# Later decodings, planning moved to the last expert, and contractions filled with zero rows

## The chip, the cores and the metric

The kernel runs on one core of a Trainium2 chip. The metric is the device time of one execution in microseconds (us); the profile shows one execution with every instruction of TensorE (PE), VectorE (DVE), ScalarE (ACT), GpSimd (POOL) and the queue engine SyncE (SP).

## The reference

Three layers follow each other: attention (a coarse one over means of four positions, and a local one over a band of seven positions), a mixture of 8 experts where each token goes to its best expert, and a dense layer with a leaky ReLU. All inputs but the two dense weights are float32; these two are float64 words.

```python
B, H, S, D = 4, 8, 576, 64
q_d, k_d, v_d = (mean of q, k, v over groups of 4 positions)      # 144 groups
out_up = np.repeat(softmax(q_d @ k_d.T / 8) @ v_d, 4, axis=2)
mask = np.abs(pos[:, None] - pos[None, :]) < 4
out_local = softmax(np.where(mask, q @ k.T / 8, -1e9)) @ v
x = (out_up + out_local) as [2304 tokens, 512]
expert_idx = argmax(normalised x @ normalised expert_emb.T / tau)
x[mask of e] = gate_w * (np.maximum(x[mask of e] @ w1[e], 0.0) @ w2[e])   # 512 -> 1024 -> 512
h = x @ w_in                                                       # 512 -> 2048
out = np.maximum(0.01 * h, h) @ w_out                              # 2048 -> 512
```

## The kernel before

**Attention.** The order of all its work, with the routing of tokens, stands in the table ORDER, one name for each step: `qk`, `vg` and `vw` load q and k, v for the means, and v for the local windows; `T`, `E`, `P` transpose q and k, copy them out of PSUM and form the means; `ds` to `dl` are the coarse attention; `S` to `LX` are the local one, in 18 tiles of 128 tokens, each of four strips of 32 positions with a window of 38 (WIN). In `lo_score` a small matmul first writes the mask into PSUM: its stationary operand is `strip4`, its moving one `mask`, with 32 rows of contraction. In `lo_pv` the contraction runs over the 38 positions of the window: exponentials are transposed in blocks of 64 columns of which 38 are used, and v is held in the tiles `vws`, of which 48 rows in each 64 are loaded. In `dn_pv` it runs over 72 groups (HG), half of 144, with exponentials in the tile deT and v in `vds`, which has a further column of ones for the sum.

**Experts.** The best expert's tokens come first, in two parts: part A (192 rows) while attention ends, part B (220 rows) after it. Then seven more follow in the order of their size, in slots of fixed capacity (372 down to 252 rows). Each expert has eight steps f; in a step `l1` makes 128 hidden units (12 matmuls), `relu` (ACT, L969) and `relu_lo` (DVE, L974) split them into a high part `hh` and a remainder `hl`, and `l2` adds their product to the output (12 matmuls). `l2` of a step stands one `l1` later. Weights are loaded by SP (`w_moe_load`) and split the same way (ACT L860, DVE L863). The rows of the next expert are gathered by POOL (`x_rows`, L759), scaled by ACT (`x_gate`, L800), transposed by PE, and split into `xhi` (ACT, L810) and `xlo` (DVE, L812) in the last four steps of the expert before.

**Planning.** Tokens beyond a slot's capacity are done in a loop at the end. The functions `pl_off` to `pl_regs` (32 small DVE instructions, L1036 to L1081) work out the places of the experts' outputs (`pl_off`) and that loop's list (all others).

**Dense weights.** They are float64 and are decoded into float32 on the chip: `w_ffn_load` (POOL queue, L883, two buffers) loads one of 32 units, `decode1` (DVE, L895 and L897) and `decode2` (DVE, L902 and L903, then a sum on POOL, L905) form the float32 words, and `w_ffn_hi` (ACT) and `w_ffn_lo` (DVE) split them. Sixteen of the units (u below 4) are decoded while experts run, the others in the dense layer.

**What sets the order behind attention.** A list `plan` of times: each step of an expert or of the dense layer has a modelled start, every function is entered with a time (`at`), and the list is sorted. The four compute engines take their instructions in that order, each engine strictly one after the other; nothing reorders on DVE, ACT, POOL or SP. Planning and decodings are entered so:

```python
            at(mid(num["e", "B", 0] + n, 6), fn, *args)          # planning, n = 0 to 7
        t0, t1 = start[num["e", "B", 0]], start[num["e", 6, 0]]
                t = t0 + (t1 - t0) * g / 16                       # unit g = 0 to 15
                at(max(start[i0] - 10.0, 1.0), w_ffn_load, u, i, j)
            at(mid(i0, 3.6), decode1, u, i, j)
```

Of the kernel before, what the change touches and what calls it, by code (L numbers as in the profile page):

```python
# [24 lines left out]
E = 8  # L25
# [31 lines left out]
ORDER = """  # L57
qk.0.0.0 ce qk.0.1.0 vg.0.1 qk.0.0.1 qk.1.1.1 emb cm qk.0.1.1 cr vg.0.0 T.0.0.0.0+8 qk.1.0.1 T.0.0.0.2 E.0.0.0.0
qk.1.1.0 K.0 T.0.0.0.1 E.0.0.0.2 T.0.1.0.0 qk.2.1.0 E.0.0.0.1 cf K.1 T.0.1.0.1 E.0.1.0.0 P.0.0.0 T.0.1.0.2 E.0.1.0.1
# [50 lines left out]
def tile_kernel(ctx, tc, q, k, v, emb, tau, w1, w2, win, wout, out):  # L110
# [51 lines left out]
    with man:  # L162
# [25 lines left out]

        vds = [ac.tile([HG, 2, H, D + 1], F32, name="vd%d" % i) for i in range(O['NVD'])]
        vws = [ac.tile([P, NP, GS, D], F32, name="vw%d" % i) for i in range(O['NVW'])]  # L190
        rep_w = ac.tile([P, 2 * HW + 4 * P], F32R, name="rep_w")
        rem_w = ac.tile([P, NP, 3 * HW], F32R, name="rem_w")

        for t in vds:
            V.memset(t[:, :, :, D:D + 1], 1.0)

        strip4 = ac.tile([STRIP, 4, STRIP], BF16, name="strip4")
        mask = ac.tile([STRIP, 3, WIN], BF16, name="mask")

# [15 lines left out]
        def consts_mask():  # L215
            G.tensor_copy(strip4, ident[:STRIP, 0:STRIP].unsqueeze(1).to_broadcast([STRIP, 4, STRIP]))
            G.memset(mask, 0.0)
            for base, sg in ((3, 1), (3, -1)):
                G.affine_select(out=mask, in_=mask, pattern=[[3 * sg, 3], [-sg, WIN]], compare_op=ALU.is_ge,
                                fill=NEG, base=base, channel_multiplier=sg)  # L220
# [103 lines left out]
        def on(kind):  # L324
            return Scalar if O["EC"][kind] == "ACT" else Vector
# [36 lines left out]
        def v_item(b, c):  # L362
            if c == 0:
                vd[b] = vds[len(vd) % O['NVD']]
            src = raw.pop((b, 2, c)).rearrange("p h (r f d) -> p r h f d", r=2, f=4)
            d = vd[b][:, :, NP * c:NP * c + NP, 0:D]
            t0 = src[:, :, :, 0, :]
            G.tensor_tensor(out=t0, in0=t0, in1=src[:, :, :, 1, :], op=ALU.add)
            G.tensor_tensor(out=d, in0=src[:, :, :, 2, :], in1=src[:, :, :, 3, :], op=ALU.add)
            G.tensor_tensor(out=d, in0=d, in1=t0, op=ALU.add)  # L370
# [39 lines left out]
        def dn_T(b, u, j):  # L410
            if j == 0:
                deT[b, u] = pl.tile([HG, 6, 2, P], F32, name="deT", tag="deT%d" % (u * O["NDE"]), bufs=1)
            e = de[b, u]
            ps = dps[b, u, j] = psB.tile([P, 512], F32, name="psDT", tag="B")
            idle(ps[:, 0:256], dn_T, b, u, j)
            for x_ in range(4):
                n, kc = 2 * j + x_ // 2, x_ % 2
                i, m = (n // 2, n % 2) if n < 4 else (n % 2, 2)
                tr(ps[:HG, x_ * P:(x_ + 1) * P], e[:, i, m, kc::2])

        def dn_Te(b, u, j):
            on('dE').copy(deT[b, u][:, 2 * j:2 * j + 2], dps.pop((b, u, j))[:HG].rearrange("p (n k g) -> p n k g", k=2, g=P))

        def dn_pv(b, u):
            eT = deT.pop((b, u))
            n_ = 4 + 2 * u
# [50 lines left out]
        def lo_score(t):  # L477
# [4 lines left out]
            for c, o in enumerate(places) if len(set(places)) > 1 else ((slice(0, P), places[0]),):  # L482
                c = c if isinstance(c, slice) else slice(32 * c, 32 * c + 32)
                for s in range(2):
                    T.matmul(ps[c, s, 0:m], strip4.rearrange("k a q -> k (a q)")[:, c],
                             mask[:, o, :].unsqueeze(1).to_broadcast([STRIP, NP, WIN]), start=True, stop=True)
            for n in range(NP):
# [46 lines left out]
        def lo_pv(t):  # L534
# [22 lines left out]
            for n in range(NP):  # L557
                for s in range(2):
                    for c, b, sg, w0 in strips(t):
                        w = vwt[b * (NSTRIP // GS) + sg // GS][:, :, sg % GS]  # L560
                        T.matmul(ps[32 * c:32 * c + 32, s, n * D:(n + 1) * D],
                                 eT[64 * s:64 * s + WIN, n, 32 * c:32 * c + 32], w[64 * s:64 * s + WIN, n, :],
                                 start=False, stop=True, skip_group_check=True)
# [537 lines left out]
        def w_half_lo(u, i, c):  # L1101
# [3 lines left out]
            es=(emb_sq,), ep=(emb_pow,), en=(emb_norm,), et=(emb_T,), emb=(load_emb,),  # L1105
            ce=(consts_escore,), cm=(consts_mask,), cf=(consts_fill,), cr=(consts_route,), qk=(load_qk,),
            vg=(load_vg,), T=(q_pe,), E=(q_ev,), P=(q_pool,), v=(v_item,), ds=(dn_score,), dm=(dn_max,),
# [47 lines left out]
        for n, (fn, args) in enumerate(((pl_off, ()), (pl_caps, ()), (pl_over, ()), (pl_tiles, ()), (pl_first, ()),  # L1155
                                        (pl_pick, (0,)), (pl_pick, (1,)), (pl_regs, ()))):
            at(mid(num["e", "B", 0] + n, 6), fn, *args)
        for i, (kind, s, f) in enumerate(steps):
# [52 lines left out]
        for g in range(32):  # L1211
            u, i, j = g // 4, g // 2 % 2, g % 2
            if u < 4:
                t = t0 + (t1 - t0) * g / 16
                i0 = max(n for n in range(len(steps)) if start[n] <= t)
                at(max(start[i0] - 10.0, 1.0), w_ffn_load, u, i, j)
            else:
# [84 lines left out]
```

## Time and profile before

| what | value |
|---|---|
| median of 3 runs | 872.42 us (865.73 to 874.82) |
| profiled execution | 870.72 us, of which 869.0 us from the first to the last instruction |
| TensorE matmul busy | 822.0 us, 95% |
| VectorE busy | 457.7 us, 53% |
| ScalarE busy | 339.7 us, 39% |
| GpSimd busy | 206.2 us, 24% |
| mean granted TensorE clock | 0.949 of full speed |

Times within the profile count from the span's first instruction. Attention runs to about 190 us, part B of the first expert from about 212 us, the other experts to about 452 us, the dense layer to the end. An engine's busy share says little by itself; what counts is which wait ends last in each stretch, and at which clock TensorE worked there.

### The profile page before, as it was taken

The page shows a single profiled execution, that of the slowest core. Times are in us where ns is not written, and L with a number is a line of the kernel's source. Part 1 is how long each engine was busy: PE and PEld are TensorE (multiplying, and loading weights), DVE is VectorE, ACT ScalarE, POOL GpSimd, SP SyncE. Part 2 cuts the span into 40 slices and gives each one's busy share as a digit, 9 for nine tenths or more (in the row PEclk, how much of TensorE's full clock was granted, in tenths as well). Part 3 has the DMA queues.
Part 4 walks back from the last instruction along what each step waited for, and adds up shares of the span by engine and source line. Part 5 has one row for each costly group of instructions (what it writes and reads, how often), then busy time and mean ns, then how long its engine had stood idle before and what let it go on. Part 6 is the DMA issues. An engine that isn't in the chain of part 4 may idle for free. (4 is left out here: it accounts for less than half of the span.)

```text
span 869.0 us, 18997 instructions
## 1 busy us (share of the span) xinstructions
PE 822.0 (95%) x7887; PEld 748.3 (86%) x7887; DVE 457.7 (53%) x901; ACT 339.7 (39%) x686; POOL 206.2 (24%) x238
## 2 busy tenths in 40 slices
PE   7979998898799999899999999999999999999995
PEld 6867877788789999899998789999999999999994
DVE  4646655263697778586659993332233232232222
ACT  3455545363345645455533332232222222232221
POOL 6555642243122433232013330101001001001001
PEclk9988978589799999999999999999999999999998
DMA  9888652556474875776653420011011011000001
GB/s 265 178 179 185 150 136 68 136 154 137 115 226 161 268 213 189 240 232 222 198 160 122 157 72 1 25 49 37 1 37 36 1 37 37 1 1 37 0 1 39
DMA packets 104652, 97.88 MB, mean 113 GB/s; under 512 B 58956, under 2 KB 83148, under 8 KB 104562
## 3 DMA queue, kind: packets, MB, share of 16 engines
q1 hardware_dynamic: 94018, 69.88, 29.0%
q0 software_dynamic: 10544, 26.74, 10.0%
q8 instruction: 64, 1.05, 0.5%
q14 instruction: 26, 0.21, 0.1%
HBM read 81.48 MB, written 15.12 MB: 111 GB/s over the span
## 5 line engine op out<-in xcount | busy, mean ns | idle before, releaser
L918 PE MATMUL psh<-xlo,w 128*128 128x384 f32 (+9 forms) x672 | 215.3, 320 | 1.9 <-DVE xlo L812 1.9
L917 PE MATMUL psh<-xhi,w 128*128 128x384 f32 (+9 forms) x672 | 215.5, 321 | 0.0
L919 PE MATMUL psh<-xhi,w 128*128 128x384 f32 (+9 forms) x672 | 214.8, 320 | 0.0
L949 DVE SCALAR_TENSOR_TENSOR hs<-hs 128x384 f32<-128x384 f32 x96 | 61.9, 645 | 186.2 <-ACT hs L948 186.2
L918 PEld LDWEIGHTS psh<-xlo,w 128*128 128x128 f32 x672 | 127.3, 189 | 6.2 <-DVE xlo L812 2.2
L917 PEld LDWEIGHTS psh<-xhi,w 128*128 128x128 f32 x672 | 127.5, 190 | 4.0
L919 PEld LDWEIGHTS psh<-xhi,w 128*128 128x128 f32 x672 | 127.2, 189 | 0.0
L948 ACT COPY hs<-psh 128x384 f32<-128x384 f32 x96 | 46.0, 479 | 194.4 <-PE psh L919 191.2
L919 PE MATMUL pso<-w,hl 128*128 128x512 f32 x282 | 112.6, 399 | 2.1 <-DVE hl L955 1.7
L917 PE MATMUL pso<-w,hh 128*128 128x512 f32 x282 | 111.7, 396 | 0.5 <-ACT hh L954 0.4
L918 PE MATMUL pso<-w,hh 128*128 128x512 f32 x282 | 111.0, 393 | 0.0
L918 PE MATMUL psy<-hl,w 128*128 128x192 f32 (+8 forms) x288 | 87.4, 304 | 10.6 <-DVE hl L974 10.5
L1021 POOL DMA_INDIRECT out_dram<-o,tk x18 | 18.5, 1025 | 320.8 <-ACT o L1020 315.1
L917 PE MATMUL psy<-hh,w 128*128 128x192 f32 (+8 forms) x288 | 89.1, 309 | 0.7 <-ACT yT L1002 0.7
L863 DVE TENSOR_TENSOR w<-r,w 128x1024 fp32r<-128x1024 f32 (+1 forms) x72 | 83.2, 1162 | 7.9 <-ACT w L860 7.6
L919 PE MATMUL psy<-hh,w 128*128 128x192 f32 (+8 forms) x288 | 87.0, 302 | 0.0
L954 ACT CAST hh<-hs 128x384 fp32r<-128x384 f32 x94 | 48.3, 513 | 92.9 <-DVE hs L949 92.9
L905 POOL TENSOR_TENSOR ds<-r 128x512 f32<-128x512 f32 x32 | 42.2, 1318 | 159.7 <-DVE r L903 85.1
L955 DVE TENSOR_TENSOR hl<-hs,hh 128x384 fp32r<-128x384 f32 x94 | 52.4, 557 | 45.8 <-ACT hh L954 45.8
L969 ACT ACTIVATE hh<-psh 128x192 fp32r<-128x192 f32 (+8 forms) x72 | 29.2, 406 | 107.3 <-PE psh L919 102.4
L919 PEld LDWEIGHTS pso<-w,hl 128*128 128x128 f32 x282 | 52.9, 188 | 20.4 <-DVE hl L955 8.5
L860 ACT CAST w<-r 128x1024 fp32r<-128x1024 f32 (+1 forms) x72 | 67.7, 948 | 6.5 <-DMA r<-in_moe_w_dram 6.5
(226 smaller groups left out, 1275.8 us busy)
## 6 DMA issues: line engine op xcount, KB each, us to landing
r<-in_moe_w_dram SPq DMA_DIRECT2D x64, 512.0 KB
r<-in_moe_w_in_dram POOLq DMA_DIRECT2D x16, 512.0 KB, 6.5
r<-in_moe_w_out_dram POOLq DMA_DIRECT2D x16, 512.0 KB, 3.7
vw<-in_v_dram SPq DMA_DIRECT2D x64, 96.0 KB
vg<-in_v_dram SPq DMA_DIRECT2D x8, 576.0 KB
x_d<-xt SPq DMA_DIRECT2D x18, 256.0 KB
yc<-yT_d SPq DMA_DIRECT2D x6, 768.0 KB
qk<-in_q_dram SPq DMA_DIRECT2D x4, 576.0 KB
```

The lines of the kernel that those rows point to most:

```text
L860: A.copy(w[:, 0, i, cs], src)
L863: V.tensor_tensor(out=w[:, 1, i, cs], in0=src, in1=w[:, 0, i, cs].bitcast(F32), op=ALU.subtract)
L905: G.tensor_tensor(out=s_.bitcast(F32), in0=lw.bitcast(F32), in1=hw.bitcast(F32), op=ALU.add)
L917: T.matmul(ps, lh, rh, start=start, stop=False)
L918: T.matmul(ps, lh, rl, start=False, stop=False)
L919: T.matmul(ps, ll, rh, start=False, stop=stop)
L948: A.copy(hs, ps[:, 0:n])
L949: V.scalar_tensor_tensor(out=hs, in0=hs, scalar=0.01, in1=hs, op0=ALU.mult, op1=ALU.max)
L954: A.copy(gh[:, 0:n], hs)
L955: V.tensor_tensor(out=gl[:, 0:n], in0=hs, in1=gh[:, 0:n].bitcast(F32), op=ALU.subtract)
L969: A.activation(hh[:, 0:n], psl1["e", s, f][:, 0:n], AF.Relu)
L1021: i = G.indirect_dma_start(out=out, out_offset=bass.IndirectOffsetOnAxis(ap=tok[c][:, j, 0:1], axis=0), in_=o, in_offset=None, bounds_chec ...
```

## The change

It has two parts. In attention, the contractions of 32, 38 and 72 rows are filled up to 128, 64 and 128 rows. The tiles `strip4`, `mask`, `vds` and deT get 128 partitions, deT becomes one tile held for the whole of attention (as a tile with one buffer it already had one place in memory), and the added rows are set to zero once, by a new step `cv` on POOL that stands third in ORDER, and by memsets of `vws` on DVE at the very start. No other name in ORDER moves.

Behind attention, planning starts three steps later with `pl_off`, and its other seven functions go to steps 1 to 7 of the last expert. The sixteen early decodings begin 18 modelled us later and are spread over what is left of the same stretch; their loads are entered 13 instead of 10 modelled us ahead.

```diff
 ORDER = """
-qk.0.0.0 ce qk.0.1.0 vg.0.1 qk.0.0.1 qk.1.1.1 emb cm qk.0.1.1 cr vg.0.0 T.0.0.0.0+8 qk.1.0.1 T.0.0.0.2 E.0.0.0.0
+qk.0.0.0 ce cv qk.0.1.0 vg.0.1 qk.0.0.1 qk.1.1.1 emb cm qk.0.1.1 cr vg.0.0 T.0.0.0.0+8 qk.1.0.1 T.0.0.0.2 E.0.0.0.0
...
-        vds = [ac.tile([HG, 2, H, D + 1], F32, name="vd%d" % i) for i in range(O['NVD'])]
+        vds = [ac.tile([P, 2, H, D + 1], F32, name="vd%d" % i) for i in range(O['NVD'])]
+        deT_ = ac.tile([P, 6, 2, P], F32, name="deT")
...
-        for t in vds:
-            V.memset(t[:, :, :, D:D + 1], 1.0)
-
-        strip4 = ac.tile([STRIP, 4, STRIP], BF16, name="strip4")
-        mask = ac.tile([STRIP, 3, WIN], BF16, name="mask")
+        for t in vws:
+            V.memset(t, 0.0)
+
+        def consts_vd():
+            for t in vds:
+                G.memset(t[64:], 0.0)
+                G.memset(t[:HG, :, :, D:D + 1], 1.0)
+            G.memset(deT_[64:], 0.0)
+
+        strip4 = ac.tile([P, 4, STRIP], BF16, name="strip4")
+        mask = ac.tile([P, 3, WIN], BF16, name="mask")
...
+            G.memset(strip4, 0.0)
+            G.tensor_copy(strip4[:STRIP], ident[:STRIP, 0:STRIP].unsqueeze(1).to_broadcast([STRIP, 4, STRIP]))
             G.memset(mask, 0.0)
...
-                             mask[:, o, :].unsqueeze(1).to_broadcast([STRIP, NP, WIN]), start=True, stop=True)
+                             mask[:, o, :].unsqueeze(1).to_broadcast([P, NP, WIN]), start=True, stop=True)
...
-                                 eT[64 * s:64 * s + WIN, n, 32 * c:32 * c + 32], w[64 * s:64 * s + WIN, n, :],
+                                 eT[64 * s:64 * s + 64, n, 32 * c:32 * c + 32], w[64 * s:64 * s + 64, n, :],
...
-            at(mid(num["e", "B", 0] + n, 6), fn, *args)
+            at(mid(num["e", "B", 3] if n == 0 else num["e", E - 1, n], 6), fn, *args)
...
-                t = t0 + (t1 - t0) * g / 16
+                t = t0 + 18.0 + (t1 - t0 - 18.0) * g / 16
                 i0 = max(n for n in range(len(steps)) if start[n] <= t)
-                at(max(start[i0] - 10.0, 1.0), w_ffn_load, u, i, j)
+                at(start[i0] - 13.0, w_ffn_load, u, i, j)
```

Three places show what this moves. The first is DVE at the begin of part B of the first expert (psx holds its transposed rows, psh its hidden units, r a loaded unit of dense weights, the names from m on belong to planning). Before:

```order
L812 TENSOR_TENSOR xlo<-psx,xhi 128x220 x4
L895 TENSOR_SCALAR ds<-r_4174 128x512
L897 SCALAR_TENSOR_TENSOR r_4174<-r_4174,ds 128x512
L974 SCALAR_TENSOR_TENSOR hl<-psh,hh 128x220
L902 TENSOR_SCALAR ds<-r_4174 128x512
L903 SCALAR_TENSOR_TENSOR r_4174<-r_4174,ds 128x512
L1036 TENSOR_TENSOR m_79<-rank,eio 128x64
L1037 TENSOR_TENSOR m_79<-m_79,cnt 128x64
L1038 TENSOR_REDUCE tmp<-m_79 128x8
L1039 CAST regs<-tmp 128x8
```

And now:

```order
L818 TENSOR_TENSOR xlo<-psx,xhi 128x220 x4
L980 SCALAR_TENSOR_TENSOR hl<-psh,hh 128x220 x4
L1042 TENSOR_TENSOR m_79<-rank,eio 128x64
L1043 TENSOR_TENSOR m_79<-m_79,cnt 128x64
L1044 TENSOR_REDUCE tmp<-m_79 128x8
L1045 CAST regs<-tmp 128x8
L980 SCALAR_TENSOR_TENSOR hl<-psh,hh 128x220
L818 TENSOR_TENSOR xlo<-psx,xhi 128x372
L869 TENSOR_TENSOR w<-r_4079,w 128x1024
```

Four remainders hl of part B stand in a row behind xlo; the decoding of r, which stood ahead of the first of them, and most of planning are gone from here.

The second is GpSimd between the gathers for the second expert (124 rows each) and for the third (112). Before:

```order
L759 DMA xe<-x_d,tks 124x512 x3
L883 DMA r_4174<-in_moe_w_in_dram 128x2x256
L883 DMA r_4176<-in_moe_w_in_dram 128x2x256
L905 TENSOR_TENSOR ds<-r_4174 128x512
L883 DMA r_4274<-in_moe_w_out_dram 128x512
L905 TENSOR_TENSOR ds<-r_4176 128x512
L883 DMA r_4448<-in_moe_w_out_dram 128x512
L759 DMA xe<-x_d,tks 112x512 x3
```

And now:

```order
L765 DMA xe<-x_d,tks 124x512 x3
L889 DMA r_4191<-in_moe_w_in_dram 128x2x256
L889 DMA r_4313<-in_moe_w_in_dram 128x2x256
L911 TENSOR_TENSOR ds<-r_4191 128x512
L765 DMA xe<-x_d,tks 112x512 x3
L889 DMA r_4422<-in_moe_w_out_dram 128x512
L911 TENSOR_TENSOR ds<-r_4313 128x512
L889 DMA r_4548<-in_moe_w_out_dram 128x512
```

The gathers for the second expert and two loads stand as they did; the gather for the third now comes after one sum of a decoding, ds, instead of two, and ahead of the third load.

The third is GpSimd at the start, behind the constants for escore. Before:

```order
L224 MEMSET escore_106 128x512
L216 CAST strip_116<-ident 32x128
L217 MEMSET mask 32x114
L219 AFFINE_SELECT mask<-mask 32x114 x2
L237 MEMSET tri 128x128
```

And now:

```order
L232 MEMSET escore_106 128x512
L200 MEMSET vd_107 64x1040
L201 MEMSET vd_107 72x16
L200 MEMSET vd_108 64x1040
L201 MEMSET vd_108 72x16
L202 MEMSET deT 64x1536
L223 MEMSET strip_118 128x128
L224 CAST strip_118<-ident 32x128
L225 MEMSET mask 128x114
L227 AFFINE_SELECT mask<-mask 32x114 x2
```

Six memsets stand ahead of the strip and the mask, and the strip and mask tiles are longer.

## Rows read from the trace of the kernel before

**Rows 1.** Windows by stage: length, busy us (instructions) per engine, clock, DMA share, GB/s

```profile
20.00:100.00 80.00, 70.72 (x1809) 58.82 (x1811) 48.51 (x110) 41.38 (x89) 42.96 (x45) 0.87 0.84 183
...
100.00:190.00 90.00, 82.35 (x2001) 70.71 (x1991) 49.03 (x168) 47.77 (x117) 35.90 (x40) 0.75 0.45 118
...
262.00:435.00 173.00, 168.99 (x1207) 167.40 (x1206) 127.84 (x192) 94.01 (x163) 46.33 (x40) 0.99 0.68 216
...
435.00:460.00 25.00, 25.00 (x185) 23.95 (x183) 15.52 (x30) 8.99 (x20) 4.16 (x6) 1.00 0.54 164
```

**Rows 2.** Waits of PE, 195 to 560 us: total us, times, longest us

```profile
PE psy L918 <- DVE hl L974: 10.5, 2, 8.7
```

**Rows 3.** Timeline of PE: start us, us, instruction, idle before it and its releaser

```profile
223.73 0.55 PE L918 MATMUL psy<-hl,w 128*128 128x220 f32 x1 [8.68 <-DVE hl L974]
...
248.01 0.68 PE L918 MATMUL psh<-xlo,w 128*128 128x372 f32 x1 [1.94 <-DVE xlo L812]
...
358.77 0.30 PE L155 MATMUL psx<-ident,xe 94*128 94x94 f32 x1 [0.65 <-ACT xe L800]
...
361.08 0.62 PE L918 MATMUL psy<-hl,w 128*128 128x300 f32 x1 [1.85 <-DVE hl L974]
```

**Rows 4.** Windows of 4 us behind the two stalls of the first expert

```profile
224.00:228.00 4.00, 4.00 (x22) 4.00 (x23) 3.60 (x12) 0.62 (x1) 1.61 (x2) 0.56 0.23 28
...
248.00:252.00 4.00, 3.99 (x18) 3.99 (x19) 3.68 (x9) 2.74 (x5) 1.48 (x2) 0.57 0.63 165
```

**Rows 5.** Timeline of DVE: decoding, first and last of planning, a later decoding

```profile
222.23 0.43 DVE L895 TENSOR_SCALAR ds<-r 128x512 uint32<-128x512 uint32 x1 [10.51 <-DMA r<-in_moe_w_in_dram]
...
222.69 0.69 DVE L897 SCALAR_TENSOR_TENSOR r<-r,ds 128x512 uint32<-128x512 uint32 x1
...
224.66 0.22 DVE L1036 TENSOR_TENSOR m<-rank,eio 128x64 f32<-128x64 f32 x1
...
249.04 0.17 DVE L1081 CAST regs<-fi 128x24 int32<-128x24 f32 x1
...
359.50 0.43 DVE L895 TENSOR_SCALAR ds<-r 128x512 uint32<-128x512 uint32 x1 [5.24 <-DMA r<-in_moe_w_in_dram]
```

**Rows 6.** DMA issues at 205.2:205.5 and 208.3:209: count, KB each, us to landing

```profile
xe<-x_d,tks POOLq DMA_INDIRECT x1, 11.6
...
r<-in_moe_w_in_dram POOLq DMA_DIRECT2D x1, 512.0 KB, 13.8
```

**Rows 7.** Windows in attention, before and in stretches of low clock

```profile
12.00:16.00 4.00, 2.23 (x46) 1.78 (x41) 2.59 (x5) 1.71 (x4) 1.90 (x4) 1.00 1.07 291
...
108.00:111.50 3.50, 3.47 (x98) 3.18 (x98) 3.29 (x11) 1.37 (x5) 2.42 (x4) 1.00 0.72 150
...
111.50:121.70 10.20, 9.77 (x188) 8.26 (x188) 2.95 (x10) 4.67 (x12) 2.20 (x3) 0.50 0.56 146
...
152.40:173.00 20.60, 17.37 (x295) 15.64 (x302) 5.40 (x23) 7.12 (x17) 4.97 (x6) 0.50 0.53 138
```

**Rows 8.** PE by line and form, 108 to 111.5 us: busy us, mean ns

```profile
L561 PE MATMUL psLV<-vw,leT 38*32 38x64 f32 x64 | 0.9, 224 | 0.0
```

**Rows 9.** PE by line and form, whole span: rows*columns, moving tile, count

```profile
L561 PE MATMUL psLV<-vw,leT 38*32 38x64 f32 x1152 | 18.1, 246 | 6.2 <-issue 6.2
...
L433 PE MATMUL psDV<-vd,deT 72*64 72x65 f32 x256 | 9.8, 229 | 1.7 <-issue 1.7
...
L553 PE MATMUL psLV<-dnl,rem_w 128*128 128x64 f32 x32 | 5.8, 308 | 0.0
```

**Rows 10.** Timeline of the start: POOL, DVE, PE

```profile
1.74 0.98 POOL L224 MEMSET escore<- 128x512 f32 x2
...
9.71 0.73 POOL L358 TENSOR_TENSOR t<-qkT 128x288 f32<-128x288 f32 x1 [1.22 <-ACT rem_w L233]
...
8.99 1.22 DVE L349 COPY qkT<-psT 128x384 f32<-128x384 f32 x2 [7.75 <-PE psT L344]
...
16.43 2.19 PE L344 MATMUL psT<-ident,qk 128*64 128x128 f32 x36 [2.20 <-DMA qk<-in_k_dram]
```

More of the change, by code (lines that the diff above doesn't have):

```diff
@@ L215, in consts_mask @@
         def consts_mask():
-            G.tensor_copy(strip4, ident[:STRIP, 0:STRIP].unsqueeze(1).to_broadcast([STRIP, 4, STRIP]))
+            G.memset(strip4, 0.0)
+            G.tensor_copy(strip4[:STRIP], ident[:STRIP, 0:STRIP].unsqueeze(1).to_broadcast([STRIP, 4, STRIP]))
             G.memset(mask, 0.0)
             for base, sg in ((3, 1), (3, -1)):
-                G.affine_select(out=mask, in_=mask, pattern=[[3 * sg, 3], [-sg, WIN]], compare_op=ALU.is_ge,
+                G.affine_select(out=mask[:STRIP], in_=mask[:STRIP], pattern=[[3 * sg, 3], [-sg, WIN]], compare_op=ALU.is_ge,
                                 fill=NEG, base=base, channel_multiplier=sg)
@@ L365, in v_item @@
             src = raw.pop((b, 2, c)).rearrange("p h (r f d) -> p r h f d", r=2, f=4)
-            d = vd[b][:, :, NP * c:NP * c + NP, 0:D]
+            d = vd[b][:HG, :, NP * c:NP * c + NP, 0:D]
             t0 = src[:, :, :, 0, :]
@@ L410, in dn_T @@
         def dn_T(b, u, j):
-            if j == 0:
-                deT[b, u] = pl.tile([HG, 6, 2, P], F32, name="deT", tag="deT%d" % (u * O["NDE"]), bufs=1)
             e = de[b, u]
@@ L421, in dn_Te @@
         def dn_Te(b, u, j):
-            on('dE').copy(deT[b, u][:, 2 * j:2 * j + 2], dps.pop((b, u, j))[:HG].rearrange("p (n k g) -> p n k g", k=2, g=P))
+            on('dE').copy(deT_[:HG, 2 * j:2 * j + 2], dps.pop((b, u, j))[:HG].rearrange("p (n k g) -> p n k g", k=2, g=P))
         def dn_pv(b, u):
-            eT = deT.pop((b, u))
+            eT = deT_
             n_ = 4 + 2 * u
@@ L1105, in tile_kernel @@
             es=(emb_sq,), ep=(emb_pow,), en=(emb_norm,), et=(emb_T,), emb=(load_emb,),
-            ce=(consts_escore,), cm=(consts_mask,), cf=(consts_fill,), cr=(consts_route,), qk=(load_qk,),
+            ce=(consts_escore,), cm=(consts_mask,), cv=(consts_vd,), cf=(consts_fill,), cr=(consts_route,), qk=(load_qk,),
             vg=(load_vg,), T=(q_pe,), E=(q_ev,), P=(q_pool,), v=(v_item,), ds=(dn_score,), dm=(dn_max,),
```

## The prediction

> **What bounds the kernel now.** I read the stages first [rows 1]; a row gives the length of the stretch, then busy time of TensorE (PE), weight load, VectorE (DVE), ScalarE (ACT) and GpSimd (POOL), the granted clock and the DMA share. From 262 us on TensorE is busy nearly without a gap (168.99 of 173 us, 25.00 of 25), so time there can come only from gaps and from the clock. From 100 to 190 us it is busy 82.35 of 90 us, but at a mean clock of 0.75: of the two levels, 2.4 and 1.2 GHz, it had the lower one for about (1 - 0.75) x 2 x 90 = 45 us, and work done there takes twice its time. From 20 to 100 us the DMA engines are 0.84 busy and TensorE idles 9.3 us; there a better clock is worth less.
>
> Second, the list of waits: behind 195 us one releaser stands out, the DVE product hl, 10.5 us in two waits [rows 2]. The timeline of TensorE puts them at 223.73 (8.68 us) and 361.08 (1.85 us, after 0.65 for gathered rows at 358.77), and a third stall, on xlo, at 248.01 (1.94 us) [rows 3]. Behind the two in the first expert the clock is low for some 3.5 us: 0.56 in 224:228, 0.57 in 248:252 [rows 4].
>
> Third, why DVE was late [rows 5]. A decoding of w_in (L895) began at 222.23 after DVE had idled 10.51 us for its load. That load was issued at 208.4 us and took 13.8 us to land [rows 6], since the next expert's weights, token gathers and two such loads were under way together. The hl that TensorE wanted stands behind the decoding in DVE's queue. The xlo of 248.01 came late for another reason: from 224.66 to 249.04 DVE also worked off the planning (L1036 to L1081, 32 instructions, 9.6 us in all), between decodings. At 359.50 a decoding waited 5.24 us for its load once more.
>
> **The change, part by part.** The sum is made against the profiled execution, 870.72 us (span 869.0 and 1.7 around it), which lies 1.7 below the median of the runs, 872.42.
>
> **Decodings begin later.** In the new order hl of the first four steps of that second part stands right behind xlo on DVE, with no decoding ahead of it. The two loads are still issued behind the same gathers and land at about 222 to 224 us as before, but are first needed at the sixth step, at about 226 us if TensorE does not stop: nothing waits for them. Gone are 8.68 us, and of the low clock behind it 4 x (1 - 0.56) = 1.8 us: 10.4 us. What is late next: at the fifth step (about 222 us instead of 233) the next expert's rows must have been gathered and its first weights landed. The second of three gathers, issued at 205.4, took 11.6 us [rows 6], so it lands at 217; the third and the weights stand between it and the load that landed at 222.2. They come between in time and 1 us late; with a clock that falls behind such a wait that is 0 to 2.7 us, and I take 0.5.
>
> **Planning moves to the last expert**, all but its first four instructions. What DVE keeps in the last steps of the first expert is what it has in every later one, where it is busy 127.84 of 173 us and TensorE hardly waits [rows 1]; so xlo comes in time. Gone are 1.94 us and 4 x (1 - 0.57) = 1.7 us; I leave 0.5 for a queue that is full. Where the planning goes there is cover: in 435:460 DVE is busy 15.52 of 25 us, so 8 to 9.6 us more fit in; without that cover they would cost at most these. On SP the reads of the planning's registers for the first expert's output now wait for the first four instructions alone.
>
> Together 10.4 + 3.7 - 1.0 = 13.1 us.
>
> **Decodings stand closer.** Sixteen of them spread over the rest of the stretch, each of them two pairs of 0.43 + 0.69 us on DVE [rows 5] and a remainder of about 0.7, so 2.9 us. Two more of them in 262:435 make DVE's 127.84 of 173 us [rows 1] 133.6, still under 0.78. Their loads get more lead in the order, but only two buffers hold them, so each is still issued behind the GpSimd sum of the one but one before, in the same queue as the gathers. The stall about 361 (0.65 and 1.85, and a low clock as behind the others: some 4 us) came when two w_in loads, a gather and output stores met. In the new order a gather stands between other loads. The stall can go or come back elsewhere: -4 to +4 us; I take -1.
>
> **Filled contractions, as work.** The instructions on TensorE stay the same in number and order. The 38-row matmuls take 246 ns each, the 72-row ones 229 [rows 9]: more rows are not longer. The nearest 128-row matmul with 64 columns has 308 ns; were that the price of depth, 18.1 x (308/246 - 1) + 9.8 x (308/229 - 1) = 8 us would be added. But it fills 128 columns where they fill 32 and 64, so I take 0, the end at which the 38- and 72-row rows stand, and keep 0 to +8.
>
> **Filled contractions, as clock.** What ran before the clock fell [rows 7]: in 108:111.5 TensorE was busy 3.47 of 3.50 us at full clock, 64 of its 98 matmuls being the 38-row ones [rows 8], and 111.5:121.7 is at 0.50. In 12:16 it was busy 2.23 of 4.00 us, with transposes of q and k that fill 128 rows in the code, and kept 1.00. So a busy TensorE lost the clock and a less busy one kept it, and the first ran shallow matmuls. The Trainium skill says otherwise ("TensorE: Matmul & The Clock Gate", Part 1, What's actually happening): the clock follows how busy TensorE has been lately. By that rule filled rows, which make no matmul longer, would leave the clock as it is and this term at 0. The trace speaks against the rule standing alone, by the two stretches just named. But it has no filled matmul to show, so I don't take the whole. The two long stretches at half clock, 111.5:121.7 and 152.4:173, hold 9.77 and 17.37 us of work: 4.9 + 8.7 = 13.6 us is the most that they give back. Inside the second TensorE stood for 3.2 us anyhow (17.37 of 20.6), and a faster TensorE meets ACT and DVE earlier. I take 6 us, somewhat under half, and keep 0 to 14.
>
> **Zeros at the start.** GpSimd gets two memsets of 64x1040, one of 64x1536 and small ones ahead of the mask. At 0.98 us for two of 128x512 [rows 10] that is 3616 columns x 0.96 ns = 3.5 us, with the rest some 4. It next had to work at 9.71 after 1.22 us of idling, so its sums come some 2.7 us late, and the scores that need them at about 14.7 instead of 13.5; TensorE then waits 2.20 us for keys until 16.43 anyhow, and this covers it. Without that cover it costs 1.2 us. DVE gets three memsets of 2304 columns behind 1.2 us; its first work is at 8.99. The trace has no long DVE memset: bounds are nothing, and the rate of the copy there (1.22 us for 2 x 384 columns, so 3.7 us each), an end at 12.2 and up to 3 us of delay, half of it ahead of the same wait for keys. The Trainium skill ("VectorE: DVE Perf Modes", Zero memsets can be issued as uint32) gives one cycle per element, by which an estimate is 2.4 us each and no delay. I take 0.3 for the whole start, near the end without delay since a memset reads nothing and the copy reads PSUM, and keep 0 to 3.
>
> **Sum:** 870.7 - 13.1 - 1 - 6 + 0.3 = 850.9, and 1.7 more for the median: 852.6. I say 852.
>
> **Rivals.**
> The clock stays: filled rows make no matmul longer and leave the clock as it is; no 6 us, so 858.6. For it: the same instructions run at the same rate. Against it: both stretches of [rows 7].
> The clock is regained in full: 14 instead of 6, so 844.6. Against it: the DMA share of 0.84 up to 100 us, and the gaps within the half-clock stretches.
> The stall only moves: the gathered rows and weights of the second expert come 3 to 4 us late and the clock falls again, and attention gains nothing: 870.7 - 7 + 1.7 = 865. For it: 13.8 us to land in that crowd.
> Slower: the denser decodings. Their place is the start of each later expert, where gather, output stores, two weight loads and now more often a decoding's load share the DMA queues. It decides when a load takes longer to land than its lead, as at 359.50; each such case costs some 4 us, since DVE holds everything behind the waiting decoding. With one at each of five experts and no better clock it is 870.7 - 13.1 + 20 + 1.7 = 879. Against it: one such stall in the whole of 262:435 now, at a DMA share of 0.68.
>
> **How the numbers follow.** Forecast 0.58, clock stays 0.21, regained in full 0.09, stall only moves 0.08, slower 0.04. The forecast's own spread is 846 to 858. With 1% (8.7 us, so 863.7) as what a measurement of this kernel can tell from none, the first three are faster, 0.88, with 0.01 of the fourth 0.89; same 0.07; slower 0.04. The range of 842 to 863 leaves out the last two and the far side of the others' spread.
>
> **What would show it.** The wait of psy on hl of 8.7 us must be gone, the decoding L895 must not wait for its load in the first expert, and the clock must be 1.00 from the end of attention to the second expert. Planning must stand in the last expert, with TensorE still without a gap there. In 100 to 190 us the clock should rise from 0.75 to about 0.83; 0.75 again means the second case. The matmuls of 38 rows, with 64, should keep about 246 ns at equal clock. I am wrong if a new wait of several us on gathered rows stands at the fifth step, or if DVE waits for w_in loads at more than one later expert.

## The result, and the profile after

The changed kernel takes 859.50 us (median of 6 runs, 853.36 to 864.60) beside 873.62 us for the kernel before on the same chip: ratio 0.9873, interval 0.9824 to 0.9922, that is 11.1 us less (6.8 to 15.4), worked out on 873.62. The ratio goes by fast runs alone, so it is not that of the two medians, which lie 14.1 us apart. The time lies in the forecast range, but the forecast of 852 expected nearly twice the gain. The profiled execution has a span of 856.2 us beside 869.0, 12.8 us less; the sum below is made on that pair.

The windows of [rows 1], after, with 212:262 beside them (length, busy us and instructions of TensorE, weight load, VectorE, ScalarE, GpSimd, then clock, DMA share, GB/s):

```profile
20.00:100.00 80.00, 67.81 (x1866) 57.71 (x1867) 48.92 (x115) 43.44 (x96) 45.01 (x47) 0.96 0.83 184
100.00:190.00 90.00, 75.27 (x1972) 65.86 (x1972) 48.84 (x171) 47.60 (x117) 36.73 (x41) 0.91 0.49 127
...
212.00:262.00 50.00, 50.00 (x358) 49.88 (x358) 36.28 (x60) 26.73 (x46) 13.50 (x12) 1.00 0.68 211
262.00:435.00 173.00, 167.77 (x1228) 165.51 (x1228) 131.88 (x221) 87.94 (x156) 46.42 (x41) 0.99 0.68 212
435.00:460.00 25.00, 21.20 (x97) 18.30 (x96) 18.86 (x33) 7.22 (x17) 7.33 (x8) 0.86 0.40 134
```

Three things stand here. The clock in attention rose from 0.87 and 0.75 to 0.96 and 0.91. The first expert and the begin of the second, 212:262, hold no gap any more (50.00 us busy, 39.38 before) and a clock of 1.00. And 435:460, which was busy without a gap, now is so for 21.20 of 25 us, at 0.86. The waits of TensorE from 190 to 460 us, in place of [rows 2]:

```profile
PE psy L923 <- ACT yT L1008: 3.8, 2, 2.0
PE pso L923 <- ACT hh L960: 3.8, 1, 3.8
PE psh L924 <- DVE xlo L818: 0.8, 1, 0.8
```

The old stalls are gone: hl of 8.7 and 1.9 us, and xlo of 1.9 us in the first expert; the waits for gathered rows fell from 1.4 to 0.5 us in sum. Of the three rows here only yT had a wait before, of 0.7 us. The timeline of TensorE says where they stand:

```profile
329.79 0.41 PE L923 MATMUL psy<-hh,w 128*128 128x300 f32 x1 [2.04 <-ACT yT L1008]
...
359.25 0.40 PE L923 MATMUL psy<-hh,w 128*128 128x282 f32 x1 [1.79 <-ACT yT L1008]
...
434.08 0.44 PE L924 MATMUL psh<-xlo,w 128*128 128x384 f32 x1 [0.79 <-DVE xlo L818]
...
446.32 0.80 PE L923 MATMUL pso<-w,hh 128*128 128x512 f32 x1 [3.81 <-ACT hh L960]
```

To see what each stage gained, I took the start of the first matmul of every stage from the timelines of both kernels (its moving tile has as many columns as the expert has rows) and the differences between them:

| stage | before, us | after, us | difference |
|---|---|---|---|
| attention, and the first expert's part A | 212.1 | 207.4 | -4.7 |
| part B (holds the stall of 8.68 us) | 32.1 | 21.4 | -10.7 |
| expert of 372 rows (holds the stall on xlo) | 36.9 | 33.1 | -3.8 |
| experts of 300 and 282 rows | 59.2 | 60.5 | +1.4 |
| experts of 336, 312, 276 and 252 rows | 109.2 | 109.0 | -0.2 |
| dense layer | 419.5 | 424.8 | +5.3 |
| span | 869.0 | 856.2 | -12.8 |

**The dense layer's 5.3 us.** Behind the wait of 3.81 us the clock is down as well:

```profile
444.00:448.00 4.00, 1.68 (x4) 1.09 (x5) 2.76 (x6) 1.89 (x4) 0.00 (x0) 0.67 0.11 33
448.00:452.00 4.00, 4.00 (x12) 3.42 (x11) 3.97 (x7) 1.03 (x2) 2.02 (x2) 0.50 0.20 51
```

The hh that TensorE waits for is made by ScalarE from hs, and hs came late; its row in ScalarE's timeline names a store as the releaser:

```profile
444.66 0.48 ACT L954 COPY hs<-psh 128x384 f32<-128x384 f32 x1 [7.24 <-DMA yT_d<-yT]
```

hs is written to a buffer that the last expert's output (yT) held until its store had landed. So the question is why the store was late, and SP's queue answers the first half of it. Its timeline and, below, its longest waits from 425 to 460 us:

```profile
434.31 0.38 SPq L848 DMA_DIRECT2D yc<-yT_d  x1
440.86 2.05 SPq L1009 DMA_DIRECT2D yT_d<-yT  x4
```

```profile
SPq L1237 <- DVE regs L1087: 12.6, 1, 12.6
SPq L1009 <- DMA yc<-yT_d: 6.0, 1, 6.0
```

The stores of the last expert's output (L1009) go to the DRAM tensor that the load of the second dense chunk (L848) reads, and stand behind it; SP waited 6.0 us for that load to land. And the load began late: 2.93 us behind the begin of the dense layer (434.31 less 431.38), before the change 1.18 us (450.65 less 449.47):

```profile
450.65 0.37 SPq L842 DMA_DIRECT2D yc<-yT_d  x1
```

Two things now stand ahead of the load. One is on SP itself: L1237 reads the number of overflow tiles and waits for planning's last instruction. Before the change SP read it in the first expert, with a wait of 6.0 us; now the read stands right ahead of the load:

```
321 L848 DMA yc<-yT_d 128x4x384
322 L851 DMA tk<-tk_d 128x3x2 x2
323 L1237 TENSOR_LOAD regs
...
325 L848 DMA yc<-yT_d 128x4x384
...
327 L1009 DMA yT_d<-yT 128x252
```

The other is on VectorE. The chunks are loaded into a tile yc that has one buffer in the program, so the load of the second chunk must wait until the fourth and last xlo of the first chunk has read it. Planning's last instruction and that xlo, then the same xlo before the change:

```profile
433.40 0.17 DVE L1087 CAST regs<-fi 128x24 int32<-128x24 f32 x1
433.48 0.55 DVE L818 TENSOR_TENSOR xlo<-yc,xhi 128x384 fp32r<-128x384 f32 x1
```

```profile
450.08 0.55 DVE L812 TENSOR_TENSOR xlo<-yc,xhi 128x384 fp32r<-128x384 f32 x1
```

The fourth xlo starts 2.10 us behind the begin of the dense layer, before the change 0.61: a decoding and planning's last five instructions stand ahead of it. The nine us up to it, after and before, with VectorE busy for 8.37 and 4.63 us of them:

```profile
425.00:434.00 9.00, 8.30 (x67) 7.97 (x65) 8.37 (x22) 2.31 (x7) 1.54 (x2) 1.00 0.01 2
```

```profile
441.00:450.00 9.00, 9.00 (x77) 9.00 (x77) 4.63 (x10) 2.76 (x7) 0.00 (x0) 1.00 0.15 37
```

So of the 1.75 us by which the load is late, 1.49 are xlo's. The load then starts 0.28 us behind the end of xlo, with SP's read in between, and 0.02 before the change: 0.26 us are SP's. The stores landed by 444.66, then ScalarE, VectorE and ScalarE again make hh, and TensorE goes on at 446.32.

**The two waits for accumulators.** At 359.25 TensorE waits until the output of the expert of 300 rows has been copied out of PSUM. GpSimd and ScalarE just ahead of it:

```profile
355.91 1.24 POOL L765 DMA_INDIRECT xe<-x_d,tks  x1 [0.30 <-issue]
357.19 1.04 POOL L911 TENSOR_TENSOR ds<-r 128x512 f32<-128x512 f32 x1
```

```profile
358.27 0.62 ACT L866 CAST w<-ds 128x512 fp32r<-128x512 f32 x1 [2.62 <-POOL ds L911]
358.79 0.71 ACT L1008 COPY yT<-psy 128x300 f32<-128x300 f32 x2
```

A decoding now falls into the last step of this expert. Its sum (L911) stands on GpSimd behind the three gathers for the next expert but one, ScalarE's split of the sum (L866) waits 2.62 us for it, and the copy of the output stands behind the split. The same happens one expert earlier, at 329.79. Behind the second the clock is 0.51 from 360 to 363.5 us. They take the place of the stall that stood at 361.08 [rows 3].

### The profile page after: what moved, and what is told of

Read it like the earlier page. It is cut to its first block, busy times and chain, and to the rows that moved or that the text cites. A ratio compares the mean times of both kernels' runs of the same rounds, so it can differ in the third digit from the quotient of the medians.

```text
span 856.2 us, 19000 instructions
## 1 busy us (share of the span) xinstructions
PE 805.8 (94%) x7887; PEld 736.6 (86%) x7887; DVE 458.7 (54%) x902; ACT 338.2 (40%) x686; POOL 211.2 (25%) x244
## 3 DMA queue, kind: packets, MB, share of 16 engines
q8 instruction: 64, 1.05, 0.6%
## 5 line engine op out<-in xcount | busy, mean ns | idle before, releaser
L923 PE MATMUL psy<-hh,w 128*128 128x192 f32 (+8 forms) x288 | 88.2, 306 | 3.8 <-ACT yT L1008 3.8
L925 PE MATMUL psy<-hh,w 128*128 128x192 f32 (+8 forms) x288 | 85.7, 297 | 0.0
L911 POOL TENSOR_TENSOR ds<-r 128x512 f32<-128x512 f32 x32 | 42.4, 1324 | 152.0 <-DVE r L909 58.9
L866 ACT CAST w<-r 128x1024 fp32r<-128x1024 f32 (+1 forms) x72 | 67.7, 948 | 1.1 <-DMA r<-in_moe_w_dram 1.1
```

The costliest lines, as they stand in the source:

```text
L866: A.copy(w[:, 0, i, cs], src)
L911: G.tensor_tensor(out=s_.bitcast(F32), in0=lw.bitcast(F32), in1=hw.bitcast(F32), op=ALU.add)
L923: T.matmul(ps, lh, rh, start=start, stop=False)
L925: T.matmul(ps, ll, rh, start=False, stop=stop)
```

## Experiments

The chips and executions differ in attention by several us, even for one program, so the text compares kernels that ran side by side on one chip, and stages of their traces where a time alone does not tell. Ratios are to the kernel before on the same chip.

**Each part alone.** pad_only has only the filled contractions (the first part of the diff of the change), order_only only the three edits of times behind attention:

```diff
-            at(mid(num["e", "B", 0] + n, 6), fn, *args)
+            at(mid(num["e", "B", 3] if n == 0 else num["e", E - 1, n], 6), fn, *args)
-                t = t0 + (t1 - t0) * g / 16
+                t = t0 + 18.0 + (t1 - t0 - 18.0) * g / 16
-                at(max(start[i0] - 10.0, 1.0), w_ffn_load, u, i, j)
+                at(start[i0] - 13.0, w_ffn_load, u, i, j)
```

> The kernel before with the filled contractions alone. If rows of zeros raise the clock, the first matmul of part A comes about 5 us earlier (188.8 to 183 or 184), the clock is about 0.96 in 20:100 and 0.91 in 100:183 instead of 0.87 and 0.75, and the time is 0.6% under the kernel before (ratio 0.994); the stall of 8.7 us on hl stays. If the clock had risen for another reason (other moments of the loads, or the new order behind attention), it stays at 0.87 and 0.75 and the ratio is 1.00.

> The kernel before with the new order of decodings and planning alone. If the two parts add up as the stages of the two traces say, attention keeps 188.8 us and a clock of 0.87 and 0.75, the two stalls of the first expert are gone (14.5 us with their clock), the dense layer loses 5.3 us, and the whole gains 7.5 us: ratio 0.991. If the dense layer's loss comes only where attention ends earlier, the gain is 13 us, ratio 0.985.

pad_only: 0.9965 (0.9924 to 1.0005). order_only: 0.9922 (0.9873 to 0.9970). The attention of both, from its begin to the first matmul of part A; order_only's is the same program as in the kernel before:

```profile
0.00:182.67 182.67, 156.41 (x4050) 133.46 (x4051) 106.62 (x285) 95.33 (x218) 94.94 (x136) 0.90 0.67 166
```

```profile
0.00:186.28 186.28, 164.40 (x4050) 139.32 (x4051) 99.18 (x284) 96.09 (x219) 90.85 (x130) 0.86 0.66 163
```

So the filling raises the clock (0.86 to 0.90; the profiles of before and after have 0.83 and 0.94), with the same matmuls in the same order, and attention is 3.6 us shorter here. By its ratio pad_only gains 3.0 us, with an interval that reaches none. Part of what attention gains is lost in the first expert's stall: beside the kernel before, the w_in load is issued 3.8 us earlier (204.60 beside 208.43) and takes as long to land, TensorE comes to the stall 5.7 us earlier, and the stall grows from 8.68 to 10.75 us:

```profile
220.10 0.55 PE L924 MATMUL psy<-hl,w 128*128 128x220 f32 x1 [10.75 <-DVE hl L980]
```

order_only takes 21.4 us for part B and 33.1 for the expert of 372 rows, just as the changed kernel does: both stalls go by the order alone. Its dense layer takes 421.7 us and pad_only's 419.4, so the dense layer's loss comes with the order, and it varies in size (2.3 us here, 5.3 above).

**Planning in the seventh expert.**

```diff
-            at(mid(num["e", "B", 3] if n == 0 else num["e", E - 1, n], 6), fn, *args)
+            at(mid(num["e", "B", 3] if n == 0 else num["e", E - 2, n], 6), fn, *args)
```

> The changed kernel with planning's last seven functions in the seventh expert instead of the eighth. Theory: SP reads the loop's count right behind planning and ahead of its load of the second dense chunk, so that load, the stores of the last expert behind it and the buffers that they free come late, which makes the wait of 3.8 us for hh, the low clock behind it and the 0.8 us for xlo. Then these go and the time falls by 5 us against the changed kernel, to about 0.982 of the kernel before. Rival: the loads of decodings that share the DMA queues with that chunk hold it up (6.0 us to land instead of 4.4); then the wait stays at 3 us or more and the time falls by 1 us at most (0.986).

0.9859 (0.9778 to 0.9940), an interval too wide to tell it from the changed kernel by time, or 0.982, the theory's figure, from 0.986, the rival's. The stages do: the dense layer takes 419.3 us. The load of the second chunk starts 1.18 us behind the begin of the dense layer, as in the kernel before, and the waits of 3.8 us for hh and 0.8 for xlo are gone:

```profile
432.84 0.37 SPq L848 DMA_DIRECT2D yc<-yT_d  x1
```

Over all profiles there is no exception: ten with planning elsewhere than in the eighth expert have a dense layer of 418.8 to 419.8 us, four with it there 421.0 to 424.8.

So planning's place is the cause; but the theory above had the wrong link. This edit takes both links away together, VectorE's work ahead of the fourth xlo and SP's read, and the traces tell them apart. In the ten the fourth xlo starts 0.60 to 0.61 us behind the begin of the dense layer and the load 0.02 to 0.03 us behind the end of xlo; in the four it is 2.09 to 2.10 and 0.28. SP's 12.6 us of waiting for the loop's count cost the load some 0.26 us, since xlo would have held it nearly as long. What the rival named, the time of that load to land, sets how much of the delay reaches TensorE: SP waited 6.0 and 6.1 us for it in the two profiles of the changed kernel, where the dense layer lost 5.3 and 4.8 us, and 4.2 and 4.4 in order_only and in dec_six below, where it lost 2.3 and 1.6. What made it land late was not tried by itself.

**Decodings kept out of an expert's last step.** dec_six moves the decoding, plan_hi (with planning in the seventh expert) only the split behind it:

```diff
                 at(start[i0] - 13.0, w_ffn_load, u, i, j)
+                if i0 % NF1 == NF1 - 1:
+                    i0 -= 1
```

```diff
-            at(mid(i0 + 1, 4.5), w_ffn_hi, u, i, j)
-            at(mid(i0 + 2, 1.5), w_ffn_lo, u, i, j)
+            i1 = i0 + (u < 4 and i0 % NF1 == NF1 - 1)
+            at(mid(i1 + 1, 4.5), w_ffn_hi, u, i, j)
+            at(mid(i1 + 2, 1.5), w_ffn_lo, u, i, j)
```

> The changed kernel with each decoding that stands in an expert's last step moved into the step before, its load left where it is. Theory: GpSimd's sum of such a decoding stands behind three gathers, ScalarE's copy of the dense weights waits for the sum and the copy of the finished expert's output stands behind that; so TensorE waits 2.0 and 1.8 us for its accumulators. With the sum ahead of the gathers both waits go, and 1.7 us of low clock with one of them: 4 to 5.5 us less than the changed kernel, ratio 0.982. Rival: the gathers, now later, become late themselves; then TensorE waits for the gathered rows instead and the time stays at 0.987.

> The changed kernel with planning in the seventh expert and, for the decodings of an expert's last step, ScalarE's and VectorE's split of the decoded weights one step later, behind the copy of the finished expert's output; GpSimd's order is that of the changed kernel. If the waits of 2.0 and 1.8 us for accumulators come from that copy standing behind the split in ScalarE's queue, they go, without the 1.8 us for gathered rows that came when the sum was put ahead of the gathers: the stretch from the expert of 300 rows to the one of 276 takes 56 us instead of 60.5. With the dense layer at 419.4 us the whole is 848 us, ratio 0.973. If the copy waits for something else (the accumulators' last matmuls, a buffer), the waits stay at 3.8 us and the ratio is that with planning moved alone, 0.98.

dec_six: 0.9886 (0.9803 to 0.9969), which is not the 0.982 expected and by time no different from the changed kernel's 0.9873; the stages tell more. The two waits for accumulators are gone, and the experts of 300 and 282 rows take 58.2 us instead of 60.5. Part of the gain turned into the rival's wait, since the gathers now stand behind the sum:

```profile
336.52 0.32 PE L155 MATMUL psx<-ident,xe 94*128 94x94 f32 x1 [1.83 <-ACT xe L806]
```

plan_hi: 0.9867 (0.9819 to 0.9916), with 0.973 expected. The waits for accumulators are gone here too, with GpSimd's order unchanged, so it was the split ahead of the copy on ScalarE that held them. But the stretch takes 58.3 us, not the 56 expected, with waits for gathered rows of 1.8 us in four pieces. The time fell less than its stages behind attention (641.0 us from part B's begin to the end, beside 648.9 in the changed kernel): attention took 190.0 us in this execution.

**Both repairs.** plan_dec has planning in the seventh expert and the decodings out of the last step.

> The changed kernel with planning in the seventh expert and the decodings of an expert's last step in the step before. If both edits add up, the dense layer takes 419.4 us and the stretch from the expert of 300 rows to that of 276 takes 58 us: 849 us, ratio 0.976. If planning in the seventh expert and the gathers of the eighth disturb each other, a wait for gathered rows of over 2 us stands there and the ratio is 0.98 or more.

0.9805 (0.9759 to 0.9852); dense layer 419.2 us, experts of 300 and 282 rows 58.4 us. The stages came as expected, the ratio as in the rival: waits for gathered rows of 2.3 us in three pieces stand there, the longest of 1.7, and attention took 189.1 us in this execution. It ran once more beside the changed kernel, together with the same kernel without any filling (plan_dec_bare) and the kernel before:

> The kernel with filled contractions, planning in the seventh expert and the decodings of an expert's last step in the step before, once more, beside the changed kernel on the same chip. If the dense layer's loss and the waits for accumulators are what the changed kernel had left, it is 5 to 8 us faster than that one: 2 to 5.3 us in the dense layer, 2 to 2.5 us between the experts of 300 and 276 rows. If not, the two are within 2 us.

> The same kernel without any filling (38, 72 and 32 rows as in the kernel before), so that the two differ in attention alone, and no stall behind attention takes up the difference. If the regained clock shortens attention as the first traces say, this one is 5 us slower (0.6%), with attention at 187 to 189 us, a clock of 0.83 to 0.87 there and TensorE busy for 164 to 168 us. If what the clock gives back is all lost to waits, as the attention of 189 to 190 us in the last two filled kernels suggests, the two are within 1.5 us, with 6 to 10 us more of TensorE's waits in the filled one.

> The changed kernel itself on this chip, with a second profile. Attention between 181 and 190 us with a clock of 0.90 to 0.94; the dense layer between 421 and 425 us, with a wait of 1 us or more for hh or xlo at its start; two waits for accumulators, of 2.0 and 1.8 us, in the experts of 300 and 282 rows.

> The kernel before itself on this chip, for a second profile of its attention. If chips and runs differ by as much as the other profiles say, attention takes 186 to 192 us at a clock of 0.83 to 0.87; the wait for hl in the first expert is 6 to 11 us.

| kernel | median, us | ratio (interval) | part A begins | part B begins | clock to part A | experts of 300, 282 rows | dense layer |
|---|---|---|---|---|---|---|---|
| before_again | 870.40 (1 run) | | 191.4 | 216.5 | 0.85 | 56.1 | 419.6 |
| after_again | 863.88 | 0.9865 (0.9826 to 0.9904) | 190.1 | 213.6 | 0.89 | 60.6 | 424.0 |
| plan_dec_again | 855.61 | 0.9808 (0.9758 to 0.9859) | 189.4 | 212.9 | 0.89 | 56.6 | 419.2 |
| plan_dec_bare | 863.63 | 0.9885 (0.9844 to 0.9926) | 195.0 | 220.0 | 0.85 | 58.3 | 419.8 |

The ratios go by 16 runs of the kernel before beside these, with a median of 876.83 us. The changed kernel repeated its result and its two losses: 3.9 us of waits for accumulators, 3.1 us for hh. Without them it is 8.3 us faster by the medians, 5.0 by the ratios (whose intervals overlap), and 638.8 beside 648.1 us from part B's begin to the end; plan_dec beats both kernels. And the filling is worth 8.0 us by the medians, 6.8 by the ratios, between two kernels that differ in the filling alone (the zero rows, the memsets that write them and the deT that is held); in the two profiles 7.1 us lie ahead of part B's begin. The attention of plan_dec_again and then of plan_dec_bare:

```profile
0.00:189.37 189.37, 164.92 (x4051) 138.93 (x4051) 106.26 (x285) 95.87 (x219) 94.75 (x136) 0.89 0.65 162
```

```profile
0.00:194.99 194.99, 168.38 (x4051) 141.37 (x4051) 100.45 (x284) 96.43 (x219) 91.03 (x130) 0.85 0.63 157
```

**Which filling?** The kernel before with one of them, its zeros and the deT that is held (the diffs are cut):

```diff
-                                 eT[64 * s:64 * s + WIN, n, 32 * c:32 * c + 32], w[64 * s:64 * s + WIN, n, :],
+                                 eT[64 * s:64 * s + 64, n, 32 * c:32 * c + 32], w[64 * s:64 * s + 64, n, :],
```

```diff
-        vds = [ac.tile([HG, 2, H, D + 1], F32, name="vd%d" % i) for i in range(O['NVD'])]
+        vds = [ac.tile([P, 2, H, D + 1], F32, name="vd%d" % i) for i in range(O['NVD'])]
+        deT_ = ac.tile([P, 6, 2, P], F32, name="deT")
```

> The kernel before with one filling alone: the local product's 38 rows become 64, with zeros in the v tiles. If the clock follows the rows filled, this one has most of it, since its 1152 matmuls are most of what ran ahead of the falls: clock in attention about 0.89 to 0.90 instead of 0.83 to 0.86 without any filling and 0.90 to 0.94 with all; TensorE's busy time there 157 to 160 instead of 164 to 168 us. If no single contraction matters, but only all together, the clock stays at 0.86 or less.

> The kernel before with one filling alone: the coarse product's 72 rows become 128, with zeros in its v and exponential tiles. If the local product carries the effect, the clock in attention stays at 0.83 to 0.87 and TensorE's busy time at 163 us or more. If depth beyond 72 matters as much (56 rows more in each of 384 matmuls, of 64 and 32 columns), the clock is 0.88 or more.

Attention of fill_local and then of fill_coarse:

```profile
0.00:189.30 189.30, 166.77 (x4050) 139.12 (x4051) 107.97 (x285) 95.83 (x219) 91.24 (x133) 0.87 0.65 162
```

```profile
0.00:188.89 188.89, 166.34 (x4050) 140.14 (x4051) 99.47 (x282) 95.69 (x219) 94.77 (x136) 0.86 0.66 162
```

Ratios 0.9995 (0.9951 to 1.0038) and 0.9988 (0.9942 to 1.0035). My expectation that the local product carries the effect failed: either alone leaves the clock at 0.87 and 0.86, while all together had 0.92 and 0.91 in plan_hi and plan_dec on this chip, with TensorE busy for 160 us. But attention is no longer in these two than in those (190.0 and 189.1 us): between these four executions the better clock went into waits, 30.0 and 28.2 us of them beside 22.5 here. Both single fillings hold deT through attention as the full one does, so that alone does not raise the clock. Whether two of the fillings suffice, and what the mask's does, was not tried.

## Why the prediction was right in direction and too large

**Decodings begin later: right.** Predicted -10.4 with 0.5 lost again, measured -10.7 in part B, which takes 21.4 us in every kernel with the new order. The clock is 1.00 through 212:262, and neither the decoding nor the next expert's rows are waited for there. Neither sign of being wrong came: from 205 to 470 us VectorE waits for no load of a decoding, where it had waited 10.51 and 5.24 us before.

**Planning leaves the first expert: right.** Predicted -3.7 with 0.5 kept back, measured -3.8 in the expert of 372 rows.

**Planning's new place: the step that failed.** "Where the planning goes there is cover: in 435:460 DVE is busy 15.52 of 25 us, so 8 to 9.6 us more fit in". The overlap was read from a mean. Over the stretch there was room, but not at the one place where it counted: in the 9 us up to the dense layer's fourth xlo VectorE is now busy for 8.37, and xlo came 1.49 us later than before. TensorE waited 0.8 us for it, and the load of the second chunk, the last expert's stores, their buffers and hh came late in turn. SP's read of the loop's count, which the working left out too (it named SP's reads of the output offsets), added some 0.26 us to the load's delay. Priced at nothing, planning's new place cost 5.3 us in the profiled pair and 1.6 to 4.8 in the others. plan_seventh shows by taking it away that the place is the cause; how the cost divides between xlo and SP's read goes by the start times alone, since no run took away one without the other.

**Decodings stand closer: sign wrong, within the bounds.** Predicted -1 with -4 to +4; measured +1.4 in the two experts concerned. The old stall near 361 went (it also went in pad_only and before_again, whose order is the old one, so it hung on the moment of the loads), and two waits for accumulators came. That the pair shows no more is due to the stall in the profile of before: over the five traces with the old order the two experts take 55.6 to 59.2 us, 56.9 in the mean, and in four with the new one 60.5 to 60.6, so the closer decodings cost some 3.6 us. I had counted the decodings' work on VectorE and their loads, not that the sum on GpSimd can fall behind three gathers, with ScalarE waiting in order for it.

**Filled contractions: size right, its parts not.** Predicted -6 + 0.3, measured -4.7 by part B in the profiled pair; in the two groups run side by side that hold bare and fully filled kernels, the means at that point differ by 3.5 us (209.7 beside 206.2) and 5.0 us (218.3 beside 213.2). As work the fillings cost nothing: the local matmul takes 224 ns at full clock in both kernels, and the mean over attention went from 246 to 241 ns [rows 9]. The clock gave back far more than I took: TensorE's busy time in attention fell from 167.72 to 152.46 us. But its idle time rose from 21.0 to 31.0 us, and that took back two thirds. Some is DMA and VectorE at the start; the largest part is the waits described in the last section. The prediction did not know of them: it gave 13.6 us as the most that comes back and took "somewhat under half" for other reasons. That more came back, and nearly as much more was lost, was luck.

The Trainium skill ("TensorE: Matmul & The Clock Gate", Part 1, What's actually happening) ties the clock to how busy TensorE has lately been. plan_dec_again and plan_dec_bare have the same matmuls in the same order and differ in rows of zeros; TensorE is busy for 0.87 and 0.86 of their attention and the clock is 0.89 and 0.85, so here the rule alone does not account for it. Over all traces the clock of attention is 0.89 to 0.94 where everything is filled (eight of them) and 0.83 to 0.86 where nothing is (four).

**Zeros at the start: right.** VectorE's three memsets are done before it is needed at 8.66 us, and TensorE's wait for keys ends at 16.32 us beside 16.43 [rows 10], with the first coarse scores (15.25) ahead of it:

```profile
1.61 1.98 DVE L196 MEMSET vw<- 128x2304 f32 x1 [0.43 <-issue]
4.01 1.98 DVE L196 MEMSET vw<- 128x2304 f32 x1 [0.43 <-issue]
6.42 1.98 DVE L196 MEMSET vw<- 128x2304 f32 x1 [0.43 <-issue]
```

They start 2.40 us apart, of which each record shows 1.98 as busy; that is between the bounds of nothing and 3.7 us each. The Trainium skill's one cycle per element ("VectorE: DVE Perf Modes", Zero memsets can be issued as uint32) gave an estimate of 2.4 us each. The trace agrees, by the 2.40 us from one start to the next.

**The sum.** -4.7 - 10.7 - 3.8 + 1.4 - 0.2 + 5.3 = -12.7, the 12.8 of the spans but for rounding. Of the 19.8 us forecast, 5.3 went to planning's new place, 2.4 to the decodings in later experts, and the rest is within the spread of attention.

## What to carry to other kernels

When work moves to a place with room, do not go by the mean of a stretch: look at what stands right behind the work in its queue, and who waits for that. Here 1.5 us of delay to one product held a load (its buffer was read last by that product), the load held stores, and the stores held buffers. A long wait on a queue says little of its cost either: of SP's 12.6 us only 0.26 counted, since the next transfer had another wait that ended nearly as late. When a long step is spread anew, look at its shortest piece too: a 1 us sum behind three gathers held a copy that TensorE needed. A gain ahead of a stall that waits for a transfer can be lost to it in part (2.1 of 5.7 us here), so judge such a gain with the stall removed.

## What was not expected of the hardware

TensorE's waits that the profile puts down to "issue" stand at fixed places of the program. In the fourteen traces those of over 0.6 us come behind the same counts of matmuls, to within one, as 854 (in all), 1491, 1999, 3272, 3399 and 3654, and the number of TensorE's records before them (matmuls, weight loads and the few of its sequencer) is 1729 plus a multiple of 256, to within one. The only other places are behind 2829 matmuls, with 0.8 and 1.1 us in two traces, and behind 2876, with 0.8 us in one. The page lists for the instruction queue q8 64 packets and 1.05 MB, 16.4 KB a packet, over a span with 15,774 matmuls and weight loads, some 246 to a packet. The times of these packets, which the traces hold, fit: each of the 76 waits at the regular places ends 1.0 to 1.75 us behind the landing of one of them, the three others 3.7 to 4.9 us. So the 76 are waits for the next piece of the instruction stream by all that the traces show; no run changed that stream. The two largest in the changed kernel:

```profile
48.54 0.79 PE L567 MATMUL psLV<-vw,leT 64*32 64x64 f32 x34 [5.35 <-issue]
163.53 0.58 PE L496 MATMUL psS<-qkT 64*32 64x38 f32 x34 [4.95 <-issue]
```

Which of these places wait, and for how long, changes from execution to execution: those over 0.6 us sum to 12.1 us in the profile of before, 21.4 in that of after, 9.6 to 17.5 in the other fully filled kernels and 9.6 to 12.5 in the other bare ones. That is a good part of the several us by which attention differs between executions, and of where the regained clock went in the first pair.
